# A gated recurrence and eight capped experts in one kernel: a new order for the last third of the stream, five units gated by GpSimd and TensorE, and three zero fills held back

## The chip, the cores and the metric

The kernel runs on one core of a Trainium2 chip. The metric is the device time of one execution in microseconds.

## What is computed

The first half is a gated linear recurrence over 4 sequences of 5056 tokens with 256 channels, the second a mixture of experts that takes the result as tokens (20224 x 256).

```python
log_a = c * sig_r * np.log(np.clip(a_base, 1e-06, 1.0 - 1e-06))[None, None, :]
a_t = np.exp(log_a)
norm = np.sqrt(np.maximum(1.0 - a_t * a_t, 1e-06))
x_gated = norm * sig_i * x
for t in range(S):
    h = a_t[:, t] * h + x_gated[:, t]
    y[:, t] = h
...
logits = x @ w_gate
expert_idx = np.argmax(logits, axis=1)
...
out = np.zeros((N, D), dtype=np.float32)
for e in range(E):
    ...
    h = np.maximum(x[tok_idx] @ w1[e], 0.0)
    out[tok_idx] = gate_w[tok_idx, None] * (h @ w2[e])
```

Each expert takes at most 80 of its tokens, those of the largest gate weight. So all but 640 rows at most of the output are zeros, and they have to be written too.

## The kernel before

**The stream.** The tokens are cut into 40 units of 512 (the last has 256). For each unit three blocks of 512 KB are loaded (tokens `Lr`, `Li`, `Lx` of the order for r_gate, i_gate and x), turned so that channels lie on partitions, and scanned. A unit goes through these steps: `Tr` transposes r on TensorE into PSUM; `tr` takes its tanh on ScalarE; `e` is the decay exp(...) on ScalarE, two instructions, one for each half of the channels; `q` squares it on GpSimd; `s` takes the root on ScalarE; `ti` is the tanh of half of i, so that the sigmoid is (1 + ti) / 2; the gating makes (1 + ti) times x, either on VectorE in one instruction (`v`, line 159) or on GpSimd in two (`u`, lines 156 and 157: add one, then multiply); `Tu` transposes the product into a PSUM tile `pu`, one for each half of the channels, four matmuls with the identity as the moving operand; `xg` multiplies it with the root on VectorE (line 167); `y` is the scan on VectorE (line 175). A digit behind a point names a half for `Tu`, `xg` and `y`, and for the others how many units one instruction takes together (`e32.2` takes units 32 and 33).

**Slots.** One large tile Y has 50 slots of 4 KB on each partition. The scans fill slots 0 to 39 for good, one for each unit; until then these and slots 40 to 49 hold what is loaded and the decays. `SLOTS` names the slot of each block. A load can't start before the last reader of what lay in its slot: for r that is `xg`, for x `Tu`, for i the gating, for a decay `y`.

**The order.** `ORDER` is one list, written out by hand, of all steps. Each engine issues its own steps in the order of this list, and SyncE its transfers: the loads, the zero fills `Z` and the weights `W`. A step that waits holds back all that stands behind it on its engine. The transfers of SyncE go to the same 16 DMA engines in the order of issue.

**Zero fills.** 40 fills of 512 KB (the last has half) write zeros to the output. All but the first copy from the part of the output that is already zero, so they read and write HBM. All 40 stand in `ORDER`; line 407 asks for what may be left, which is nothing.

**Routing.** `G` makes the logits of four units (16 matmuls), `R s.k` are the steps of routing group s (maximum, exp, key, sum, reciprocal, gate weight, store). `P` takes the largest cells of a stretch, `M` merges them. `M0` (line 349) also replaces the eight largest and finds the next eight. `F` are matmuls that only keep TensorE running.

**Weights.** Slots 40 to 47 become the buffers of two experts' weights. `W0` to `W3` load the halves of w1 of experts 0 and 1, `W4` to `W7` those of w2. In the list W0 comes first, then W7, W3, W6, W5, W4, W2 and W1, with four fills between them; nine fills stand behind W1.

**Selection and experts.** After line 407 the 80 best tokens of each expert are chosen, mostly on VectorE. `experts()` then runs a loop over k from -1 to 7: in step k TensorE makes the first products of expert k + 1 (line 629) and the second ones of expert k (line 631), in two halves of the inner dimension. Behind each half SyncE issues the next weights of the buffers just read: `load_w1(e1 + 2, half)` and `load_w2(e2 + 2, half)`. The w1 of expert 2 is first used in step 1, its w2 and the w1 of expert 3 in step 2.

Of the kernel before, what the change touches and what calls it, by code (L numbers as in the profile page):

```python
# [13 lines left out]
ALU = mybir.AluOpType  # L14
# [14 lines left out]
SLOTS = dict(r=(14, 25, 30, 35, 38, 18, 21, 16, 34, 9, 11, 20, 13, 26, 25, 37, 42, 45, 40, 48, 41, 49, 22, 31, 24, 30, 44, 45, 41, 46, 49, 35, 32, 37, 42, 46, 44, 45, 41, 46),  # L29
             i=(34, 40, 4, 27, 37, 44, 23, 37, 28, 19, 15, 23, 32, 18, 46, 49, 38, 16, 21, 30, 28, 25, 26, 34, 37, 32, 43, 36, 38, 31, 36, 30, 41, 45, 36, 43, 49, 37, 38, 49),  # L30
             x=(20, 12, 29, 22, 40, 24, 6, 42, 36, 29, 27, 35, 41, 24, 36, 17, 29, 18, 27, 43, 33, 38, 47, 42, 33, 28, 32, 27, 34, 38, 33, 34, 48, 33, 38, 48, 40, 43, 40, 47),
             a=(15, 8, 31, 19, 33, 5, 14, 7, 17, 10, 30, 12, 28, 34, 14, 23, 35, 38, 19, 20, 27, 35, 23, 29, 25, 26, 40, 47, 28, 29, 43, 31, 40, 47, 34, 35, 36, 42, 48, 39))
# [51 lines left out]
def moe_kernel(ctx, tc, x, r_gate, i_gate, a_param, w_gate, w1, w2, out, capacity=80):  # L84
# [129 lines left out]
    for k in range(6): nc.gpsimd.memset(tiny[:, 70 + k % 4:71 + k % 4], 0.0)  # L214
# [171 lines left out]
    def weights(w):  # L386
# [4 lines left out]
             'Tr': r_transposes, 'tr': r_tanh, 'e': decay, 'q': square, 's': root, 'ti': i_tanh, 'u': gated, 'v': gated,  # L391
# [15 lines left out]
    zero_fill(-(-N // ZERO_TOKENS))  # L407
# [180 lines left out]
    def experts(arm):  # L588
        fstack = ExitStack()
# [31 lines left out]
        def products(e1, e2, half):  # L621
# [17 lines left out]
            if e1 is not None and e1 + 2 < E: load_w1(e1 + 2, half)  # L639
            if e2 is not None and e2 + 2 < E: load_w2(e2 + 2, half)  # L640
# [80 lines left out]
```

## Time and profile before

| | |
|---|---|
| time, median of 3 runs | 292.08 us (287.35 to 293.74) |
| the profiled execution's own time | 287.59 us |
| its span, first to last instruction | 285.9 us |
| mean granted TensorE clock, share of full speed | 0.915 |
| busy: VectorE, ScalarE, GpSimd, TensorE | 223.0, 232.9, 213.0, 211.1 us |
| DMA, mean rate over the span | 352 GB/s |

The shares are means over three stages that have different limits: the stream to about 201 us, the selection to about 223 us and the experts to the end. PE is TensorE's matmuls, PEld its weight loads, DVE VectorE, ACT ScalarE, POOL GpSimd, SP SyncE. A clock of 1.00 is 2.4 GHz, 0.50 is 1.2 GHz.

### The profile page before, as it was taken

The numbers are of one execution on the slowest core, as the hardware profiler recorded it, in microseconds if no ns is written. First come the engines' busy times: TensorE is split into PE (matmuls) and PEld (weight loads), VectorE is DVE, ScalarE is ACT, GpSimd is POOL, SyncE is SP. The second block draws the span as 40 slices with busy tenths as digits, with TensorE's granted clock in tenths as the row PEclk, the third lists the DMA queues.
The fourth block names the chain that finished last, engine by engine and source line by source line (L and its number), as shares of the span: only waits on it lengthen the run. The fifth ranks groups of instructions, "written<-read, shape, count | busy, mean of one in ns | idle before, by whom it ended". The sixth has DMA issues, their size and how long they took to land.

```text
span 285.9 us, 5799 instructions
## 1 busy us (share of the span) xinstructions
PE 211.1 (74%) x1488; PEld 161.0 (56%) x1488; DVE 223.0 (78%) x506; ACT 232.9 (81%) x488; POOL 213.0 (75%) x372
## 2 busy tenths in 40 slices
PE   2635849598556985479857696486787889999995
PEld 2634723375444354462555325333676779999994
DVE  2018999999999999999999999999995663445510
ACT  7999999999999999999999999999264754544400
POOL 3279488789999999999999788998375682816521
PEclk9995977689959999779979997979999997999999
DMA  6999999999999999999889999999999997999831
GB/s 232 417 386 416 410 408 408 409 391 396 411 405 436 367 367 359 386 344 413 318 318 396 353 406 387 410 364 344 304 408 406 347 297 240 342 340 331 299 93 32
DMA packets 32825, 100.74 MB, mean 352 GB/s; under 512 B 3744, under 2 KB 12576, under 8 KB 32160
## 3 DMA queue, kind: packets, MB, share of 16 engines
q1 hardware_dynamic: 32400, 99.64, 93.1%
q0 software_dynamic: 384, 0.66, 0.7%
q8 instruction: 14, 0.23, 0.3%
q14 instruction: 27, 0.22, 0.2%
HBM read 99.10 MB, written 21.36 MB: 421 GB/s over the span
## 4 chain that ended last, share of the span: by engine, by line
DMA 29%; PE 21%; DVE 17%; POOL 12%; ACT 8%; issue 8%; SPq 2%; ACTq 1%; DVEq 0%; POOLq 0%
DMA Y<-in_x_dram 11%; PE po L631 9%; PE ph L629 7%; DVE Y L175 6%; POOL Y L157 6%; DMA Y<-in_i_gate_dram 6%; DMA Y<-in_r_gate_dram 6%; DMA Y<-in_moe_w_dram 4%; POOL Y L145 3%; DVE Y L159 3%; DMA Y<-in_moe_w_gate_dram 3%; DVE pu L167 3%; POOL Y L156 2%; ACT Y L142 2%; SPq L120 2%
## 5 line engine op out<-in xcount | busy, mean ns | idle before, releaser
L175 DVE TENSOR_TENSOR_SCAN Y<-Y,pu 128x512 f32<-128x512 f32 (+4 forms) x86 | 97.9, 1171 | 0.4
L164 PE MATMUL pu<-ident,Y 128*128 128x128 f32 x316 | 53.7, 303 | 49.0 <-DVE Y L175 26.0
L145 POOL TENSOR_TENSOR Y<-Y 128x1024 f32<-128x1024 f32 (+2 forms) x29 | 74.5, 2589 | 18.8 <-ACT Y L142 17.6
L164 PEld LDWEIGHTS pu<-ident,Y 128*128 128x128 f32 x316 | 38.7, 154 | 71.3 <-issue 37.9
L157 POOL TENSOR_TENSOR Y<-Y 128x1024 f32<-128x1024 f32 (+1 forms) x23 | 57.4, 2498 | 1.9
L128 PE MATMUL pr<-ident,Y 128*128 128x128 f32 x316 | 50.1, 313 | 11.5 <-DMA Y<-in_r_gate_dram 8.2
L128 PEld LDWEIGHTS pr<-ident,Y 128*128 128x128 f32 x316 | 43.5, 165 | 16.4 <-issue 6.7
L167 DVE SCALAR_TENSOR_TENSOR pu<-Y,pu 128x512 f32<-128x512 f32 (+1 forms) x80 | 51.2, 673 | 0.6 <-ACT Y L148 0.2
L142 ACT ACTIVATE Y<-Y,tiny 128x1024 f32<-128x1024 f32 (+2 forms) x48 | 49.5, 1089 | 0.1
L631 PE MATMUL po<-Y,rows 128*80 128x128 f32 x256 | 46.9, 279 | 0.0
L629 PE MATMUL ph<-Y 128*128 128x80 f32 x256 | 43.1, 263 | 2.7 <-DMA Y<-in_moe_w_dram 1.8
L629 PEld LDWEIGHTS ph<-Y 128*128 128x128 f32 x256 | 38.1, 196 | 3.4 <-POOL Y L617 3.3
L152 ACT ACTIVATE Y<-Y 128x1024 f32<-128x1024 f32 (+2 forms) x30 | 39.6, 1328 | 0.4 <-DMA Y<-in_i_gate_dram 0.3
L130 ACT ACTIVATE Y<-pr 128x1024 f32<-128x1024 f32 (+1 forms) x40 | 39.4, 1009 | 0.1
L616 ACT COPY Y<-Y 128x2 f32 x256 | 25.8, 191 | 16.7 <-issue 14.2
L148 ACT ACTIVATE Y<-Y 128x2048 f32<-128x2048 f32 (+2 forms) x26 | 37.5, 1493 | 0.4 <-POOL Y L145 0.2
L159 DVE SCALAR_TENSOR_TENSOR Y<-Y 128x1024 f32<-128x1024 f32 (+1 forms) x16 | 23.8, 1500 | 16.2 <-DMA Y<-in_moe_w_gate_dram 10.1
L617 POOL COPY Y<-Y 128x2 f32 x192 | 24.6, 195 | 14.7 <-DVE Y L646 5.7
L238 PE MATMUL pl<-Y 128*32 128x512 f32 x144 | 34.1, 1077 | 0.5 <-DVE Y L175 0.5
L156 POOL TENSOR_SCALAR Y<-Y 128x1024 f32<-128x1024 f32 (+1 forms) x23 | 26.6, 1158 | 6.0 <-ACT Y L152 5.7
L631 PEld LDWEIGHTS po<-Y,rows 128*80 128x80 f32 x256 | 29.2, 155 | 0.0
L643 DVE TENSOR_SCALAR rows<-ph 128x320 f32<-128x320 f32 x8 | 3.9, 492 | 27.1 <-PE ph L629 24.0
(165 smaller groups left out, 200.3 us busy)
## 6 DMA issues: line engine op xcount, KB each, us to landing
Y<-in_r_gate_dram SPq DMA_DIRECT2D x39, 512.0 KB, 6.9
Y<-in_i_gate_dram SPq DMA_DIRECT2D x39, 512.0 KB, 7.2
Y<-in_x_dram SPq DMA_DIRECT2D x39, 512.0 KB, 7.7
out_dram<-out_dram SPq DMA_DIRECT2D x38, 512.0 KB, 9.6
Y<-in_moe_w_dram SPq DMA_DIRECT2D x32, 512.0 KB, 6.9
out_dram<-Y SPq DMA_DIRECT2D x1, 512.0 KB, 10.4
Y<-in_x_dram SPq DMA_DIRECT2D x1, 256.0 KB, 5.7
Y<-in_i_gate_dram SPq DMA_DIRECT2D x1, 256.0 KB, 5.1
```

Of the source, the lines that this page charges most:

```text
L128: nc.tensor.transpose(pr[:, h, b:nb * P:nb], rr[:, b, h * P:(h + 1) * P], ident)
L130: nc.scalar.activation(rslot(u), prs.pop(u)[:, :, :ntok(u)], AF.Tanh, scale=0.5)
L142: nc.scalar.activation(a[:, :, h], z[:, :, h], AF.Exp, scale=L[:, h:h + 1], bias=L[:, h:h + 1])
L145: nc.gpsimd.tensor_tensor(pair('r', u, m), a, a, op=ALU.mult)
L148: nc.scalar.activation(q, q, AF.Sqrt, scale=-0.25, bias=0.25)
L152: nc.scalar.activation(i, i, AF.Tanh, scale=0.5)
L157: nc.gpsimd.tensor_tensor(v, i, v, op=ALU.mult)
L164: nc.tensor.transpose(pu[:, b:nb * P:nb], tmb('x', u)[:, b, h * P:(h + 1) * P], ident)
L167: nc.vector.scalar_tensor_tensor(pu, rslot(u)[:, h], 0.5e-3, pu, op0=ALU.max, op1=ALU.mult)
L175: nc.vector.tensor_tensor_scan(y[:, s0:s1], a[:, s0:s1], q[:, s0:s1], init, op0=ALU.mult, op1=ALU.add)
L629: if e1 is not None: nc.tensor.matmul(ph[:, c % (FC // 2)], w1v(e1)[:, h, c * P:c * P + P], XG[:, e1, h], start=(h == 0), stop=(h == 1))
L631: if e2 is not None: nc.tensor.matmul(po[:, h, :P], h2T[:, c], w2v(e2)[:, c, h * P:h * P + P], start=(c == 0), stop=(c == FC - 1))
```

## The change

The list is the same up to unit 26. Behind it all steps of units 27 to 39 are in a new order, and 39 of the slots are others; of those, r36 goes to slot 47, x36 to 41 (behind x34), x38 to 44, r39 to 47 (behind r36), i39 to 41 (behind x36) and x39 to 48 (behind i37).

Units 30, 32, 34, 36 and 38 are gated by a new step `w`: GpSimd multiplies ti with x in one instruction, and `Tu` sums the transposes of x and of that product in PSUM, eight matmuls a half in place of four. Before, four of these units were gated by GpSimd (`u`) and unit 34 by VectorE (`v34.1`).

The decays of units 37 and 38 and the roots of 35 and 36 are made together (`e37.2`, `s35.2`). The step `R4.4` moves behind the last scan, and `M4` takes over the replacing and the second search from `M0`, behind `R5.2`.

Of the 40 fills 33 stand in the list, four follow at line 407, and three wait until the first weights of expert 2 have been issued: one behind the first half, two (the half-size one is among them) behind the second. The weights come in the order W0, W4, W5, W2, W1, W3, W6, W7. Six more one-column memsets stand at the start of GpSimd's work.

```diff
@@
 GATHER = (32, 24, 24)
 STEPS = ((0, 1), (2, 3), (4, 5), (6, 7), (8,), (9,))
...
@@
-    Tu27.1 xg26.1 y26.0 y26.1 xg27.1 Lr32 Tu27.0 Lr36 Lx30 xg27.0 Tr31 s29.2 Tu28.1 R2.4 s28.1 y27.1 y27.0 Li33 Z R2.5 xg28.1 Tu28.0 Tr32 xg28.0
-    Tu29.1 y28.1 Lx31 tr31 y28.0 Li32 u30.1 R2.6 xg29.1 Z R2.7 tr32 Tr33 Tu29.0 e31.1 xg29.0 Tu30.0 Tr36 y29.1 tr33 Lr35 ti31.1 e32.2 y29.0 R2.8
-    Tu30.1 v31.1 q31.1 ti32.2 q32.2 Li34 Lx34 xg30.0 R2.9 Tu31.0 xg30.1 Lx33 Tr35 Li36 y30.0 Z s31.1 y30.1 P2 s32.2 Z xg31.0 tr35 Li35 Tu31.1
-    u32.1 xg31.1 u33.1 ti34.1 G6 Lr38 y31.0 Tu32.0 Tu32.1 e34.2 y31.1 Lx35 xg32.0 xg32.1 y32.0 Z G7 Tu33.0 tr36 v34.1 R3.0 q34.2 ti35.2 y32.1
-    Tu33.1 xg33.0 xg33.1 e36.1 q36.1 R3.1 R3.2 Lr37 R3.3 y33.1 v35.1 s34.1 Z Z Lx36 Tu34.0 y33.0 R3.4 R3.5 Li37 u36.1 xg34.0 Tu34.1 xg34.1 Tr37
-    s35.1 s36.1 tr37 ti37.1 Lx37 y34.0 Tu35.1 Tu35.0 Tr38 Lx39 e37.1 y34.1 xg35.1 R3.6 Z R3.7 R3.8 xg35.0 y35.1 tr38 Li38 u37.1 R3.9 y35.0 e38.1
-    Tu36.1 P3 Tu36.0 Z Li39 Z Lr39 G8 ti38.1 xg36.1 Tu37.1 xg36.0 y36.1 y36.0 q37.1 q38.1 s37.1 Lx38 Z xg37.1 R4.0 Tu37.0 s38.1 R4.1 xg37.0 R4.2
-    R4.3 y37.0 Tr39 ti39.1 u38.1 Tu38.1 Z Z Z Z y37.1 Z u39.1 Z tr39 e39.1 q39.1 R4.4 Tu38.0 I0 xg38.1 Ga0 Z xg38.0 W0 Z s39.1 y38.1 y38.0 Tu39.0
-    Tu39.1 xg39.1 R4.5 xg39.0 W7 y39.1 Z Ga1 W3 W6 W5 W4 Z Z Ca y39.0 Gb F R5.0 R4.6 M0 R5.1 W2 R4.7 W1 Z Z R4.8 M1 M3 Z F F F F F R5.2 F F F F I1 Z Z Z R4.9 Z R5.3 Z
-    R5.4 Z R5.5 R5.6 R5.7 R5.8 F F F F F F F F M2 R5.9
+    Tu27.1 xg26.1 y26.0 xg27.1 Tu27.0 y26.1 Tu28.0 xg27.0 Tr33 Li32 y27.1 s28.2 R2.4 R2.5 xg28.0 y27.0 s30.1 y28.0 Tu28.1 ti31.1 Tr31 R2.6 Lx30
+    Lr32 Tu29.0 Lx31 tr31 Li33 xg28.1 Lr36 R2.7 Tu29.1 xg29.1 xg29.0 R2.8 w30.1 tr33 e31.1 y28.1 q31.1 Tr32 tr32 R2.9 Tu30.0 e32.2 Lx34 ti32.2
+    y29.0 Tu30.1 q32.2 xg30.0 v31.1 y30.0 G6 s31.1 y29.1 xg30.1 Tu31.1 Tu31.0 Tr36 Lr35 Z Lx33 y30.1 Tr35 Li36 Li34 Z w32.1 xg31.1 xg31.0 u33.1
+    s32.2 tr35 y31.1 ti34.1 y31.0 Tu32.0 Tu32.1 G7 xg32.0 e34.2 tr36 Li35 w34.1 R3.0 Z Lx35 xg32.1 y32.0 y32.1 Tu33.1 Tu33.0 q34.2 Tu34.0 ti35.2
+    R3.1 Li37 P2 xg33.1 xg33.0 Z Lr37 y33.1 Tu34.1 e36.1 R3.2 v35.1 Lr38 Lx36 R3.3 y33.0 Lx37 R3.4 s34.1 xg34.1 q36.1 xg34.0 Tu35.0 R3.5 R3.6
+    y34.0 Tr37 R3.7 Tr38 Tu35.1 s35.2 Z ti37.1 y34.1 xg35.0 xg35.1 Z y35.0 w36.1 tr37 R3.8 tr38 Tu36.1 R3.9 e37.2 Li38 u37.1 ti38.1 Z Lx38 y35.1 Z
+    q37.1 Tu36.0 xg36.1 G8 xg36.0 Tu37.0 s37.1 q38.1 y36.1 Lr39 R4.0 y36.0 s38.1 P3 Li39 ti39.1 Tu37.1 Lx39 xg37.0 Z Z xg37.1 y37.0 Tr39 tr39
+    w38.1 Z R4.1 Z Z Tu38.1 R4.2 y37.1 xg38.1 Z Tu38.0 Ga0 xg38.0 u39.1 y38.1 e39.1 Tu39.0 W0 q39.1 Tu39.1 s39.1 W4 y38.0 xg39.0 R4.3 Z Ga1 xg39.1
+    y39.0 Z y39.1 I0 Ca Gb F R5.0 R4.4 R4.5 R4.6 M0 R5.1 W5 W2 W1 W3 R4.7 R5.2 Z Z R4.8 M1 M4 M3 Z F F F F F F F F F I1 Z Z Z R4.9 R5.3 Z R5.4 Z
+    R5.5 R5.6 R5.7 R5.8 F F F F F F F F W6 W7 M2 R5.9
 """
 EARLY = 8
+HELD = (1, 2)
 class Plan:
@@
         for token in ORDER.split():
             kind = token.rstrip("0123456789.")
             self.order.append((kind, *map(int, filter(None, token[len(kind):].split(".")))))
-        self.by_pool = {u + k for kind, *a in self.order if kind == 'u' for u in a[:1] for k in range(a[1])}
+        self.by_pool, self.summed = ({u + k for kind, *a in self.order if kind == g for u in a[:1] for k in range(a[1])} for g in 'uw')
         self.steps = STEPS
         self.step_of = {g: s for s, gs in enumerate(STEPS) for g in gs}
@@
             nc.gpsimd.tensor_tensor(v, i, v, op=ALU.mult)
         else:
             nc.vector.scalar_tensor_tensor(v, i, 1.0, v, op0=ALU.add, op1=ALU.mult)
+    def times_tanh(u, m):
+        ti, v = flat_pair('i', u, m), flat_pair('x', u, m)
+        nc.gpsimd.tensor_tensor(ti, ti, v, op=ALU.mult)
     def u_transposes(u, h):
+        terms = [tmb(k, u) for k in ('xi' if u in plan.summed else 'x')]
         pu = pus[u, h] = ps_u.tile([P, C], F32, name="pu")
         nb = ntok(u) // P
         for b in range(nb):
-            nc.tensor.transpose(pu[:, b:nb * P:nb], tmb('x', u)[:, b, h * P:(h + 1) * P], ident)
+            for n, v in enumerate(terms):
+                nc.tensor.matmul(pu[:, b:nb * P:nb], v[:, b, h * P:(h + 1) * P], ident, start=(n == 0), stop=(n == len(terms) - 1), is_transpose=True)
     def normed(u, h):
         n = ntok(u); pu = pus[u, h][:, :n]
         nc.vector.scalar_tensor_tensor(pu, rslot(u)[:, h], 0.5e-3, pu, op0=ALU.max, op1=ALU.mult)
@@
     cidx = tiny[:, 38:70]; ecol = tiny[:, 22:38]
     nc.gpsimd.iota(cell0, pattern=[[2 * P, 4]], base=0, channel_multiplier=0, allow_small_or_imprecise_dtypes=True)
     warm = tiny[:, 21:22]
-    for k in range(6): nc.gpsimd.memset(tiny[:, 70 + k % 4:71 + k % 4], 0.0)
+    for k in range(12): nc.gpsimd.memset(tiny[:, 70 + k % 4:71 + k % 4], 0.0)
     dio = tiny[:, 4:20]
     for e in range(2 * E): nc.gpsimd.memset(dio[:, e:e + 1], float(E - e % E))
@@
             nc.gpsimd.iota(nth, pattern=[[1, NC]], base=0, channel_multiplier=0, allow_small_or_imprecise_dtypes=True)
             best(0)
             find(0)
+        if n == 4:
             nc.vector.match_replace(cell, rows[:, NE:NE + 8], cell, -1.0)
             best(8)
         pool = nc.gpsimd
@@
         load(e, g)
     tasks = {'Lr': lambda u: load('r', u, rf), 'Li': lambda u: load('i', u, jf), 'Lx': lambda u: load('x', u, xf),
-             'Tr': r_transposes, 'tr': r_tanh, 'e': decay, 'q': square, 's': root, 'ti': i_tanh, 'u': gated, 'v': gated,
+             'Tr': r_transposes, 'tr': r_tanh, 'e': decay, 'q': square, 's': root, 'ti': i_tanh, 'u': gated, 'v': gated, 'w': times_tanh,
              'Tu': u_transposes, 'xg': normed, 'y': scan, 'G': logits, 'R': lambda s, k: stages[k](s), 'Ga': logits_first, 'Gb': logits_last, 'Ca': copy_first, 'P': cell_top, 'M': merge, 'I': prepare, 'W': weights, 'Z': lambda: zero_fill(1), 'F': filler}
     with tc.manual_schedule(engines={E_.Activation, E_.PE, E_.DVE, E_.Pool}):
         for n, (kind, *args) in enumerate(plan.order):
@@
     sel = bank[:5 * E, :CAP]
     tstack = ExitStack()
     ps_t = tstack.enter_context(tc.tile_pool(name="ps_t", bufs=1, space=bass.MemoryType.PSUM))
-    zero_fill(-(-N // ZERO_TOKENS))
+    zero_fill(-(-(N - nz[0]) // ZERO_TOKENS) - sum(HELD))
+    filled = nz[0]
     KG, KF = -(-CAP // 8) * 8, 14
     chosen = small[:5 * E, 0:CAP]
@@
     _, fv = nc.values_load_multi_w_load_instructions(flag, engines=[E_.PE, E_.DVE, E_.Activation, E_.Pool, E_.SP], min_val=0, max_val=P,
                                                      skip_runtime_bounds_check_because="a count of rows")
     def experts(arm):
+        nz[0] = filled
         fstack = ExitStack()
         tstack = ExitStack()
         ps_t = tstack.enter_context(tc.tile_pool(name="ps_a" + arm, bufs=1, space=bass.MemoryType.PSUM))
@@
             for c in cs[len(lone):]:
                 for h in range(2): first(c, h); second(c, h)
             if e1 is not None and e1 + 2 < E: load_w1(e1 + 2, half)
+            if e1 == 0: zero_fill(HELD[half])
             if e2 is not None and e2 + 2 < E: load_w2(e2 + 2, half)
         def relu(e, half):
             dst = hbuf[e % 2].rearrange("p (c s) -> p c s", c=FC)[:, half * FC // 2:(half + 1) * FC // 2]
```

## Rows read from the trace of the kernel before

**Rows 1.** Stage windows: busy us of PE, PEld, DVE, ACT, POOL; clock, DMA share, GB/s.

```profile
160.00:170.00 10.00, 9.16 (x52) 3.07 (x52) 9.97 (x14) 9.94 (x10) 9.36 (x5) 1.00 0.98 383
230.00:240.00 10.00, 8.21 (x67) 8.01 (x67) 6.58 (x57) 5.15 (x49) 4.79 (x38) 0.85 0.98 321
260.00:270.00 10.00, 10.00 (x101) 10.00 (x100) 4.71 (x40) 5.83 (x54) 6.98 (x43) 1.00 0.99 330
```

**Rows 2.** Chain of waits, 215 us to the end: start, us, what.

```profile
225.67 10.57 DMA Y<-in_moe_w_dram
```

**Rows 3.** TensorE timeline around the experts' first matmuls; in brackets the idle time before.

```profile
223.66 1.98 PE L629 MATMUL ph<-Y 128*128 128x80 f32 x16 [0.94 <-ACT Y L616]
...
236.38 0.42 PE L629 MATMUL ph<-Y 128*128 128x80 f32 x2 [1.79 <-DMA Y<-in_moe_w_dram]
```

**Rows 4.** Two-microsecond windows, columns as in the first group.

```profile
222.00:224.00 2.00, 1.06 (x7) 0.66 (x6) 1.32 (x12) 1.67 (x18) 0.85 (x7) 1.00 1.04 369
238.00:240.00 2.00, 2.00 (x12) 2.00 (x12) 0.42 (x4) 0.00 (x0) 0.00 (x0) 0.50 0.93 323
```

**Rows 5.** SyncE timeline: start, us, line, transfers issued.

```profile
185.47 0.33 SPq L120 DMA_DIRECT2D Y<-in_x_dram  x1
185.86 6.10 SPq L230 DMA_DIRECT2D out_dram<-out_dram  x8
196.84 0.39 SPq L381 DMA_DIRECT2D Y<-in_moe_w_dram  x1
...
211.42 12.57 SPq L230 DMA_DIRECT2D out_dram<-out_dram  x9
225.67 5.86 SPq L381 DMA_DIRECT2D Y<-in_moe_w_dram  x3
231.62 0.88 SPq L384 DMA_DIRECT2D Y<-in_moe_w_dram  x1
...
241.28 0.37 SPq L381 DMA_DIRECT2D Y<-in_moe_w_dram  x1
...
244.52 0.37 SPq L381 DMA_DIRECT2D Y<-in_moe_w_dram  x1
```

**Rows 6.** DMA issues at 185.47, 196.84, 225.67, 231.62 us; last number: us to landing.

```profile
Y<-in_x_dram SPq DMA_DIRECT2D x1, 512.0 KB, 6.0
...
Y<-in_moe_w_dram SPq DMA_DIRECT2D x1, 512.0 KB, 9.4
...
Y<-in_moe_w_dram SPq DMA_DIRECT2D x1, 512.0 KB, 10.6
...
Y<-in_moe_w_dram SPq DMA_DIRECT2D x1, 512.0 KB, 8.6
```

**Rows 7.** VectorE timeline, 168 to 196 us.

```profile
169.20 1.41 DVE L159 SCALAR_TENSOR_TENSOR Y<-Y 128x1024 f32<-128x1024 f32 x1
...
194.56 0.28 DVE L300 SCALAR_TENSOR_TENSOR pl<-pl,tiny 128x128 f32<-128x128 f32 x1
```

**Rows 8.** GpSimd timeline, 160 to 168 us.

```profile
162.44 1.05 POOL L156 TENSOR_SCALAR Y<-Y 128x1024 f32<-128x1024 f32 x1
163.57 2.42 POOL L157 TENSOR_TENSOR Y<-Y 128x1024 f32<-128x1024 f32 x1
```

**Rows 9.** TensorE timeline, 185 to 196 us.

```profile
185.99 3.81 PE L238 MATMUL pl<-Y 128*32 128x512 f32 x16 [0.54 <-DVE Y L175]
...
194.31 1.09 PE L164 MATMUL pu<-ident,Y 128*128 128x128 f32 x8 [2.31 <-POOL Y L157]
```

**Rows 10.** ScalarE groups by form, 130 to 201 us: count, busy, mean ns.

```profile
L142 ACT ACTIVATE Y<-Y,tiny 128x512 f32<-128x512 f32 x10 | 7.6, 810 | 0.0
```

**Rows 11.** GpSimd groups by form, first 10 us: count, busy, mean ns, idle before.

```profile
L145 POOL TENSOR_TENSOR Y<-Y 128x1024 f32<-128x1024 f32 x1 | 1.9, 1892 | 7.0 <-ACT Y L142 7.0
...
L214 POOL MEMSET tiny<- 128x1 f32 x6 | 0.3, 88 | 0.0
```

**Rows 12.** Page, under the DMA queues.

```profile
HBM read 99.10 MB, written 21.36 MB: 421 GB/s over the span
```

More of the change, by code (lines that the diff above doesn't have):

```diff
@@ L28 @@
 STEPS = ((0, 1), (2, 3), (4, 5), (6, 7), (8,), (9,))
[L29 to L32, printed above, removed]
+SLOTS = dict(r=(14, 25, 30, 35, 38, 18, 21, 16, 34, 9, 11, 20, 13, 26, 25, 37, 42, 45, 40, 48, 41, 49, 22, 31, 24, 30, 44, 45, 41, 46, 37, 43, 48, 49, 42, 46, 47, 40, 45, 47),
+             i=(34, 40, 4, 27, 37, 44, 23, 37, 28, 19, 15, 23, 32, 18, 46, 49, 38, 16, 21, 30, 28, 25, 26, 34, 37, 32, 43, 36, 38, 33, 35, 38, 32, 33, 37, 35, 38, 48, 42, 41),
+             x=(20, 12, 29, 22, 40, 24, 6, 42, 36, 29, 27, 35, 41, 24, 36, 17, 29, 18, 27, 43, 33, 38, 47, 42, 33, 28, 32, 48, 31, 36, 45, 31, 34, 45, 41, 43, 41, 37, 44, 48),
+             a=(15, 8, 31, 19, 33, 5, 14, 7, 17, 10, 30, 12, 28, 34, 14, 23, 35, 38, 19, 20, 27, 35, 23, 29, 25, 26, 40, 47, 28, 29, 30, 36, 40, 44, 34, 36, 49, 43, 46, 39))
 ORDER = """
```

## Prediction

> **What bounds the kernel now.** I read the stage windows first, then the chain of waits, then the place it points to on TensorE, SyncE and the DMA rings. In the stream VectorE and ScalarE are busy for 9.97 and 9.94 of 10 us, GpSimd for 9.36, and the DMA share is 0.98, so four things are nearly full together and an edit to one of them can be eaten by the next [rows 1]. In the last experts TensorE is busy without a gap while the DMA engines move 330 GB/s at the pace at which TensorE frees the weight buffers [rows 1]. Between the two lies the only long DMA piece of the chain's last third: 10.57 us from 225.67 us [rows 2]. It is the first half of expert 2's w1, issued when TensorE has read expert 0's. TensorE needs it at 236.38 - 1.79 = 234.59 us and waits 1.79 us [rows 3]. Then the clock stands at 0.50, 1.2 GHz, in the window 238 to 240 us, although it was 1.00 around the shorter idle time of 0.94 us before the first product [rows 3, 4]. SyncE's issues mark the ends of the halves: the half that began at 236.38 ended at 241.28 (4.90 us), the next at 244.52 (3.24 us) [rows 3, 5]. So the low clock cost 4.90 - 3.24 = 1.66 us. **Wait and clock together cost 3.45 us**, and that is what holding fills back aims at.
>
> The weight comes late because of what is queued ahead of it: nine fills, issued over 12.57 us from 211.42 us [rows 5]. I price the queue by landings, issue plus time to landing [rows 5, 6]: x38, the last load, 185.47 + 6.0 = 191.5; W0 196.84 + 9.4 = 206.2; the weight in question 225.67 + 10.6 = 236.3; the first half of expert 2's w2 231.62 + 8.6 = 240.2. Between the last two only weights run, the last included three: 3.9 / 3 = **1.3 us a weight**. Between x38 and W0 lie eight fills and one weight: (14.7 - 1.3) / 8 = 1.68 us a fill. Between W0 and 236.3 lie eight weights and 12.5 fills: (30.1 - 10.4) / 12.5 = 1.58. I take **1.6 us a fill**.
>
> **The change: the stream.** VectorE loses `v34`, 1.41 us [rows 7]. GpSimd loses four additions of 1.05 and gains one product of 2.42, 1.8 us less in sum [rows 8]. ScalarE loses part of four decay instructions of 0.81 us, at most two of them, 1.6 us, and at least nothing [rows 10]. TensorE gets 5 x 8 = 40 more transposes; eight take 1.09 us, so 5.5 us over some 40 us [rows 9]. It has the time: it stood waiting 2.31 us for GpSimd's product before one such group [rows 9]. On the path, behind a product that comes late, each half costs 1.09 / 2 = 0.55 us more. `M4` and the three instructions of `R4.4` (0.28 us for the first) only move on VectorE, to where it is the bound anyway; I cost them at nothing, and at 0.9 us if VectorE was idle where `R4.4` stood, since it filled a gap before `xg38` there [rows 7]. The six memsets cost 6 x 0.088 = 0.5 us of GpSimd before its first product, where it idles 7.0 us: nothing [rows 11].
>
> So the stream can end 1.4 us earlier at best. Against that stand three new waits. `R3.6` now stands right behind `xg34`, before GpSimd has surely finished `R3.5`. `G8`'s 3.81 us stand on TensorE before `Tu37`, and VectorE has only `y36` and `P3` to fill them [rows 9]. A `w` has nothing to do before x has landed, while the addition in `u` needed only ti. The bounds are a gain of 1.4 and a loss of 0.6 us: two halves of `Tu` uncovered, 1.1, and the 0.9 of `R4.4`'s gap, against the 1.4. I take a gain of 0.6: 1.4 less one uncovered half, 0.55, less the first 0.28 of that gap. Nothing in the selection changes, so TensorE needs expert 2's first weight at 234.0 us.
>
> **The fills and the weights.** What counts is what runs after the last load. Before: 8 + 12.5 fills and nine weights to the end of the weight in question. After: six fills ahead of W0, then two, eight and four, 20 in all, and the same nine weights. Only half a fill less, 0.8 us, although three are held back: the list has seven fills fewer, but the four of line 407 still come ahead of the weight, and they were taken out of the stream. The rest of the saving, two fills, lies ahead of the last load, and it counts only if the DMA engines don't run dry there. The two bounds: all 2.5 fills count, 236.3 - 2.5 x 1.6 = 232.3; or the last load lands when it did, 236.3 - 0.8 = 235.5. I take **235.0**, near the second, because the last load is now x39, whose slot is freed by GpSimd's `u37` and not by the queue, with r39 and i39 waiting for unit 36 just ahead of it on SyncE. So the first wait is 235.0 - 234.0 = 1.0 us, close to the 0.94 us that left the clock alone, and I count no low clock for it.
>
> Then the held fills are due: one behind the first half, 1.5 behind the second. Expert 2's w2 lands behind 2.5 fills and three weights, 235.0 + 4.0 + 3.9 = 242.9. TensorE would be there at 235.0 + 2 x 3.24 = 241.5, so **a new wait of 1.4 us** takes the place of the old one. Step 2 starts at 242.9 and started at 244.52. From there on TensorE's pace decides as before. The first scatter has to follow the held fills, and GpSimd's copies for a later expert stand behind it on that engine; the fills land ahead of expert 2's w2, in time for both. The sum: 242.9 - 244.52 = -1.6 us on 287.59 us (span 285.9, 1.7 around it): **286.0 us**. If the clock falls in the second wait, it is 1.66 us more, 287.6. The median shown, 292.08, is 4.5 us above the profiled execution and the shortest run (287.35); my sum stands on the profiled one, and runs like the median's would put the change near 290.5.
>
> A word on the price of a fill. The row says 421 GB/s of HBM traffic, read and written, over the whole span [rows 12]. The Trainium skill, "DMA: Bandwidth & Descriptors", section Specifications, gives about 358 GB/s as the limit of HBM for one core and says that this side binds. By that, a fill that reads and writes 0.52 MB each would take 1.05 MB / 358 GB/s = 2.9 us, an estimate from the page, and my sum would get 2.5 x 1.3 = 3.3 us longer. The trace goes past that limit, so the row decides.
>
> **The rivals.** *Both waits gone.* The queue never runs dry: the weight lands at 232.3, and expert 2's w2 at 232.3 + 7.9 = 240.2; the stream gives its whole 1.4 us, TensorE is ready at 233.2 and at 239.7 and waits 0.5 us at most. 240.2 - 244.52 = -4.3: 283.3 us. For it speaks the DMA share of 0.98 in the stream, against it that loads wait for slots, not for the queue [rows 1]. *Nothing gained.* The first wait stays near 1.5 us or the second comes to as much, the clock falls, 287.6 us. The change then doesn't do what its words say: the fills are held back, but only as many as were put off from the list into the stretch ahead of the weight. *Slower: late x.* x36 now takes slot 41, freed by the second `Tu34`, where it had one that was free after a scan two units earlier. GpSimd's `w36` waits for it, with `u37`, `q37`, `q38`, `w38` and `u39` queued behind, x39 waits for `u37`, and on SyncE all last fills and weights wait behind x39. Loads took 6.0 us to land there and up to 10.6 under a full queue [rows 6]. If x36 lands 3 us after GpSimd has come to `w36`, stream and weight both move by 3 us: 286.0 + 3.0 = 289.0 us. It decides from 1.6 us on, where the gain is used up. *Dear fills.* Beside weights a held fill could cost more than in a run of fills; at 2.9 us each step 2 starts 3.3 us later, 289.3 us.
>
> **How the numbers follow.** Forecast 286.0 (284.5 to 287.2) 0.42; both waits gone 0.22; nothing gained 0.18; late x 0.13; dear fills 0.05. The range reaches from below the second to above the fourth, with the median's distance in view: 282.5 to 290.5. Two per cent, 5.8 us, is about what a measurement here can tell from no change, since the three runs lie 6.4 us apart. Faster by more needs 281.8: only a tail of the second case and the scatter of the runs, 0.15. Slower by more needs 293.3: 0.06. Within: 0.79.
>
> **What would show it.** In the profile after: the 1.79 us wait of line 629 before step 1 shrinks to about 1 us or goes, with no stretch at 0.50 behind it; a wait for line 384's or 381's load appears before step 2; the weight behind the fills lands near 235 us; VectorE's last scan ends 0.2 to 1.4 us earlier. I am wrong if the first product of the experts starts later than 223.7 us (then the stream lost), if no wait stands before step 2 (then fills are cheaper or the queue ran ahead), or if the clock is low for more than the 1.66 us.

## Result: 1.1 per cent slower, where 0.6 per cent faster was forecast

The changed kernel takes 289.9 us (median of 20 runs, 288.15 to 292.27), the kernel before in the same series 289.19 us (median of 20, 286.25 to 294.71). The ratio is **1.0108, 95% interval 1.0085 to 1.0131**; it is larger than that of the medians because disturbed runs, of which the kernel before had more, are left out of it. The profiled execution took 290.63 us, 3.0 us more than the one before, where 1.6 us less was forecast.

**The profile after.** The stage windows answer to [rows 1]. In the stream VectorE is busy for 9.70 of 10 us in place of 9.97 and GpSimd for 9.92 in place of 9.36; where the experts start, TensorE is busy for 6.46 in place of 8.21.

```profile
160.00:170.00 10.00, 9.51 (x64) 4.78 (x56) 9.70 (x12) 9.94 (x9) 9.92 (x5) 1.00 0.96 354
230.00:240.00 10.00, 6.46 (x55) 6.26 (x54) 6.46 (x57) 5.16 (x49) 4.81 (x38) 0.86 0.98 335
260.00:270.00 10.00, 10.00 (x102) 10.00 (x101) 6.87 (x52) 5.15 (x49) 7.37 (x50) 1.00 1.04 337
```

The rest is read from the end of the stream to the start of the experts. VectorE's timeline first, one row of before and four of after: the last scan started 0.68 us earlier, but the three instructions of `R4.4`, which had stood ahead of `xg38`, now stand behind it.

```profile
199.61 1.38 DVE L175 TENSOR_TENSOR_SCAN Y<-Y,pu 128x256 f32<-128x256 f32 x2
...
198.93 1.38 DVE L181 TENSOR_TENSOR_SCAN Y<-Y,pu 128x256 f32<-128x256 f32 x2
200.22 0.27 DVE L306 SCALAR_TENSOR_TENSOR pl<-pl,tiny 128x128 f32<-128x128 f32 x1
200.53 0.29 DVE L307 TENSOR_REDUCE Y<-pl 128x16 f32<-128x128 f32 x1
200.85 0.29 DVE L308 TENSOR_TENSOR lg<-pl,Y 128x128 f32<-128x128 f32 x1
```

What follows `R4.4` on VectorE started at 201.06 us, so `R4.4` took 0.84 us; before, the same instruction started at 200.90, so the gain was given back. TensorE's timeline shows the first product of the experts 0.05 us earlier than in [rows 3], and the wait that was to shrink is twice as long:

```profile
223.61 1.98 PE L638 MATMUL ph<-Y 128*128 128x80 f32 x16 [0.92 <-ACT Y L625]
...
238.09 0.69 PE L638 MATMUL ph<-Y 128*128 128x80 f32 x2 [3.54 <-DMA Y<-in_moe_w_dram]
```

In the chain of waits the weight is one DMA piece, as in [rows 2], 1.76 us longer:

```profile
225.62 12.33 DMA Y<-in_moe_w_dram
```

SyncE's timeline, to compare with [rows 5]: the last load, the fills (line 236), the weights (388 w1, 391 w2), and, from 244.21 us on, the issues that mark the ends of the experts' halves.

```profile
188.33 0.33 SPq L121 DMA_DIRECT2D Y<-in_x_dram  x1
188.71 4.62 SPq L236 DMA_DIRECT2D out_dram<-out_dram  x6
195.64 0.39 SPq L388 DMA_DIRECT2D Y<-in_moe_w_dram  x1
196.13 0.43 SPq L391 DMA_DIRECT2D Y<-in_moe_w_dram  x1
196.61 1.21 SPq L236 DMA_DIRECT2D out_dram<-out_dram  x2
197.92 0.53 SPq L391 DMA_DIRECT2D Y<-in_moe_w_dram  x1
199.20 2.88 SPq L388 DMA_DIRECT2D Y<-in_moe_w_dram  x3
203.67 11.37 SPq L236 DMA_DIRECT2D out_dram<-out_dram  x8
216.26 2.15 SPq L391 DMA_DIRECT2D Y<-in_moe_w_dram  x2
219.60 4.62 SPq L236 DMA_DIRECT2D out_dram<-out_dram  x4
225.62 0.37 SPq L388 DMA_DIRECT2D Y<-in_moe_w_dram  x1
...
233.53 0.37 SPq L391 DMA_DIRECT2D Y<-in_moe_w_dram  x1
...
244.21 0.37 SPq L388 DMA_DIRECT2D Y<-in_moe_w_dram  x1
...
247.44 0.37 SPq L388 DMA_DIRECT2D Y<-in_moe_w_dram  x1
```

The half behind the wait runs from 238.09 to 244.21, 6.12 us in place of 3.23 for the next, so the low clock cost 2.89 us, against 1.66 before. Two-microsecond windows (columns of [rows 1]) show it: 0.50, 1.2 GHz, after TensorE had stood idle for 3.54 us.

```profile
238.00:240.00 2.00, 1.91 (x10) 1.94 (x11) 0.40 (x4) 0.00 (x0) 0.00 (x0) 0.50 1.06 412
240.00:242.00 2.00, 2.00 (x12) 2.00 (x12) 0.00 (x0) 0.00 (x0) 0.00 (x0) 0.50 0.94 358
242.00:244.00 2.00, 2.00 (x13) 2.00 (x12) 0.00 (x0) 0.00 (x0) 0.17 (x1) 0.50 0.75 274
244.00:246.00 2.00, 2.00 (x21) 2.00 (x21) 0.00 (x0) 1.72 (x16) 1.65 (x7) 0.99 0.73 214
```

**The account:** first product -0.05, wait 3.54 - 1.79 = +1.75, low clock 2.89 - 1.66 = +1.23: +2.9 of the 3.0 us. The landings behind it, in the form of [rows 6], for the issues at 188.33 (x39), 195.64 (W0), 225.62 and 233.53 us:

```profile
Y<-in_x_dram SPq DMA_DIRECT2D x1, 256.0 KB, 4.2
...
Y<-in_moe_w_dram SPq DMA_DIRECT2D x1, 512.0 KB, 8.0
...
Y<-in_moe_w_dram SPq DMA_DIRECT2D x1, 512.0 KB, 12.3
...
Y<-in_moe_w_dram SPq DMA_DIRECT2D x1, 512.0 KB, 11.6
```

x39 landed at 192.5 us, W0 at 203.6, the weight at 237.9. Between the last two lie 14 fills and eight weights, at the prediction's 1.3 us a weight (34.3 - 10.4) / 14 = 1.71 us a fill.

Ahead of x39 the DMA engines had room. SyncE issued nothing from 181.56 to 187.08 us, since r39's slot wasn't free; before, the longest pause in the 25 us ahead of x38 was 3.45 us. Windows of before, of after and of experiment 3, which has four fills more ahead of x39; the last two figures are DMA share and GB/s:

```profile
172.00:186.00 14.00, 7.65 (x48) 6.18 (x50) 13.90 (x20) 13.94 (x16) 12.34 (x11) 0.87 0.98 390
...
172.00:186.00 14.00, 8.99 (x60) 7.67 (x58) 13.90 (x20) 13.94 (x14) 12.14 (x10) 0.88 0.92 334
...
172.00:186.00 14.00, 9.98 (x61) 9.21 (x60) 13.90 (x20) 13.94 (x15) 10.66 (x10) 0.76 0.99 404
```

In the windows of two microseconds in it the share of after swings between 0.64 and 1.37. So the engines didn't stand still throughout, but over these 14 us they moved 0.8 MB less than before, 1.5 fills.

### The profile page after: what moved, and what is told of

The parts are those of the page before. It is cut to its first block, busy times and chain, and to the rows that moved or that the text cites. A ratio compares the mean times of both kernels' runs of the same rounds, so it can differ in the third digit from the quotient of the medians.

```text
span 288.9 us, 5876 instructions
## 1 busy us (share of the span) xinstructions
PE 217.7 (75%) x1528; PEld 168.3 (58%) x1528; DVE 222.2 (77%) x505; ACT 232.4 (80%) x485; POOL 211.2 (73%) x375
## 4 chain that ended last, share of the span: by engine, by line
PE 23%; DMA 21%; POOL 18%; DVE 18%; issue 11%; ACT 6%; SPq 2%; ACTq 1%; POOLq 0%; DVEq 0%
DMA Y<-in_x_dram 9%; PE po L640 9%; PE ph L638 7%; POOL Y L146 6%; DVE Y L181 5%; POOL Y L158 5%; DMA Y<-in_moe_w_dram 4%; DVE pu L173 4%; DVE Y L160 3%; DMA Y<-in_moe_w_gate_dram 3%; DMA Y<-in_i_gate_dram 3%; PE pl L244 3%; POOL Y L157 2%; PE pu L170 2%; POOL Y L163 2%
## 5 line engine op out<-in xcount | busy, mean ns | idle before, releaser
L181 DVE TENSOR_TENSOR_SCAN Y<-Y,pu 128x512 f32<-128x512 f32 (+5 forms) x86 | 98.2, 1172 | 0.5
L170 PE MATMUL pu<-ident,Y 128*128 128x128 f32 x356 | 59.6, 305 | 47.8 <-DVE Y L181 24.3
L170 PEld LDWEIGHTS pu<-ident,Y 128*128 128x128 f32 x356 | 44.3, 156 | 70.5 <-issue 37.2
L129 PEld LDWEIGHTS pr<-ident,Y 128*128 128x128 f32 x316 | 44.2, 167 | 12.3 <-issue 6.0
L158 POOL TENSOR_TENSOR Y<-Y 128x1024 f32<-128x1024 f32 (+1 forms) x19 | 47.9, 2520 | 1.6
L143 ACT ACTIVATE Y<-Y,tiny 128x1024 f32<-128x1024 f32 (+2 forms) x46 | 48.8, 1122 | 0.1
L638 PE MATMUL ph<-Y 128*128 128x80 f32 x256 | 44.0, 268 | 4.5 <-DMA Y<-in_moe_w_dram 3.5
L638 PEld LDWEIGHTS ph<-Y 128*128 128x128 f32 x256 | 39.0, 200 | 5.1 <-issue 3.7
L160 DVE SCALAR_TENSOR_TENSOR Y<-Y 128x1024 f32<-128x1024 f32 (+1 forms) x15 | 22.8, 1531 | 15.9 <-DMA Y<-in_moe_w_gate_dram 10.1
L157 POOL TENSOR_SCALAR Y<-Y 128x1024 f32<-128x1024 f32 (+1 forms) x19 | 22.4, 1178 | 6.6 <-ACT Y L153 5.3
```

What stands on the lines that cost most here:

```text
L129: nc.tensor.transpose(pr[:, h, b:nb * P:nb], rr[:, b, h * P:(h + 1) * P], ident)
L143: nc.scalar.activation(a[:, :, h], z[:, :, h], AF.Exp, scale=L[:, h:h + 1], bias=L[:, h:h + 1])
L170: nc.tensor.matmul(pu[:, b:nb * P:nb], v[:, b, h * P:(h + 1) * P], ident, start=(n == 0), stop=(n == len(terms) - 1), is_transpose=True)
L181: nc.vector.tensor_tensor_scan(y[:, s0:s1], a[:, s0:s1], q[:, s0:s1], init, op0=ALU.mult, op1=ALU.add)
L638: if e1 is not None: nc.tensor.matmul(ph[:, c % (FC // 2)], w1v(e1)[:, h, c * P:c * P + P], XG[:, e1, h], start=(h == 0), stop=(h == 1))
```

## The experiments

**Theory A, the queue:** the list has seven fills fewer. Three of them had stood behind W0 and are held back now. Four had stood ahead of W0, in the stream, where the DMA engines now have room; they come at line 407, in the stretch ahead of expert 2's first weight, and holding back three (2.5 by size) doesn't make up for these four. (The expectation of 1 speaks of seven fills taken out of the stream; by the lists it is four.) Rivals: **B**, the new order or the gating loses; **C**, W6 and W7, now last, delay the weight; **D**, only the first weight counts, so more held fills would cure it. Times are told by the ratio to the kernel before on the same chip. From each profiled execution I take one number that leaves the stream out, product to end: span less the start of the experts' first product (all in us).

| kernel | ratio to before (95%) | first product | span | product to end |
|---|---|---|---|---|
| before | 1 | 223.66 | 285.9 | 62.2 |
| after | 1.0108 (1.0085 to 1.0131) | 223.61 | 288.9 | 65.3 |
| 1 held alone | 0.9887 (0.9812 to 0.9963) | 224.19 | 285.9 | 61.7 |
| 1 again | 0.9916 (0.9871 to 0.9962) | 225.27 | 283.8 | 58.5 |
| 2 none held | 1.0172 (1.0114 to 1.0231) | 224.11 | 291.6 | 67.5 |
| 3 four back | 0.9949 (0.9915 to 0.9982) | 224.68 | 283.1 | 58.4 |
| 3 again | 0.9945 (0.9901 to 0.9988) | 226.40 | 284.8 | 58.4 |
| 4 three back | 0.9924 (0.9881 to 0.9967) | 225.01 | 283.5 | 58.5 |
| 5 seven held | 1.0101 (1.0037 to 1.0164) | 223.99 | 289.9 | 65.9 |
| 6 W6, W7 early | 1.0058 (1.0015 to 1.0101) | 224.42 | 290.3 | 65.9 |
| 7 kept busy, 28 | 1.0110 (1.0072 to 1.0148) | 224.33 | 288.8 | 64.5 |
| 8 kept busy, 14 | 1.0020 (0.9971 to 1.0068) | 223.71 | 287.7 | 64.0 |
| 9 old gating | 1.0155 (1.0064 to 1.0246) | 232.10 | 293.7 | 61.6 |
| 10 held, warmer | 0.9926 (0.9879 to 0.9972) | 229.38 | 287.8 | 58.4 |

**1. Three fills held back in the kernel before, and nothing else.** The list loses three `Z` at its end.

```diff
+HELD = (1, 2)
...
+            if e1 == 0: zero_fill(HELD[half])
```

Expected: 

> The kernel before with nothing but the held fills: the last three of its nine fills behind W1 leave the list and go behind the halves of expert 2's w1, as in the change. Theory A (the queue decides: the change lost because its list gave seven fills out of the stream into the stretch ahead of expert 2's first weight, and holding three back doesn't make up for that): the weight lands 2.5 x 1.6 = 4.0 us earlier, near 232.3 us, TensorE doesn't wait for it, no window at 0.50 follows, and the time falls by the whole 3.45 us of wait and low clock, to about 284 us in a run like the profiled one. Theory B (the new order and gating of the stream cost the time, the fills matter little): within 1 us of the kernel before.

Measured: 287.16 us (median of 6), before 288.38; -1.1 per cent, as A has it. No wait for a weight was left: the first half of expert 2's w1 was issued at 226.20 and landed 6.4 us later. But the clock fell all the same, in the second half of step 0 and without a long wait ahead of it (TensorE, then windows; the same 16 matmuls take 2.01 us at full clock):

```profile
224.19 1.98 PE L632 MATMUL ph<-Y 128*128 128x80 f32 x16 [0.78 <-ACT Y L619]
...
226.34 3.42 PE L632 MATMUL ph<-Y 128*128 128x80 f32 x16
```

```profile
228.00:230.00 2.00, 2.00 (x12) 2.00 (x12) 0.65 (x6) 1.40 (x15) 0.80 (x7) 0.50 0.84 262
230.00:232.00 2.00, 2.00 (x11) 2.00 (x11) 1.80 (x16) 0.88 (x9) 2.00 (x17) 0.50 0.77 268
```

**1 again**, on another chip. Expected: 

> The kernel before with the three held fills once more, for the comparison with two more keep-running matmuls on the same chip: the ratio to the kernel before again near 0.989, times spread over 4 to 5 us. If the clock's fall at 228 us is a matter of one execution, this profile shows 1.00 there, and its span is 2 to 2.5 us shorter than 285.9.

Measured: 286.43 us (12 runs), before 288.77. This profile has no low clock there, and 58.5 us from product to end, 3.2 less than the first:

```profile
228.00:230.00 2.00, 2.00 (x20) 2.00 (x20) 1.73 (x16) 2.00 (x21) 0.97 (x8) 1.00 0.80 217
```

So the fall belongs to single executions, not to this kernel; 58.4 to 58.5 us is the price of the experts when nothing waits and the clock holds.

**2. The change with no fill held back**, `HELD = (0, 0)`, so that seven stand at line 407. Expected: 

> The changed kernel with all seven fills issued ahead of expert 2's first weight, none held back. A: the weight lands 2.5 x 1.7 = 4.3 us later than in the changed kernel, near 242 us, the wait grows from 3.5 to about 7.8 us, the time by 4 us, to about 294. B: no change beyond 1 us.

Measured: 293.54 us (6 runs). TensorE's wait:

```profile
242.23 0.69 PE L638 MATMUL ph<-Y 128*128 128x80 f32 x2 [7.26 <-DMA Y<-in_moe_w_dram]
```

Three fills more ahead of the weight, one of them half-size, put it 4.1 us later, 1.7 us for a full one. A's place and size hold.

**3. The change with the four fills of line 407 back in the stream**, where the engines had room: one behind `Lr36`, two behind `Lr38`, one behind the last fill ahead of `Lr39`. Of each line only the place that differs:

```diff
-    Lr36 R2.7
+    Lr36 Z R2.7
...
-    Lr38 Lx36 R3.3
+    Lr38 Z Z Lx36 R3.3
...
-    Lx38 y35.1 Z
+    Lx38 y35.1 Z Z
```

Expected: 

> The changed kernel with the four fills of line 407 put back into the list of the stream: one behind Lr36, two behind Lr38, one behind the last fill before Lr39; three stay held. A: there the DMA engines had gaps, so the last loads come at most 1 us later, and the weight lands 4 x 1.7 - 1 = 5.8 us earlier, near 232.2 us; the wait of 3.54 us and the 2.9 us of low clock both go, and the time falls to about 283.5 us, under both kernels. B: the fills get in the way of the loads of units 36 to 39, the stream ends later, and the time stays at 290 us or more.

Measured: 285.88 us (12 runs), before 288.38. The weight was issued at 226.70 and landed at 231.7, 6.2 us earlier than in the change, no product waited for it, and the clock was 1.00 from 214 to 252 us:

```profile
Y<-in_moe_w_dram SPq DMA_DIRECT2D x1, 512.0 KB, 5.0
```

x39, issued at 188.33 as in the change, took 6.7 us and not 4.2, and the first product came 1.07 us later. That the four fills cost this is not shown: in 5, with no fill put back, x39 took 6.8 us, and in 6, whose stream is the change's, the first product came 0.81 us later than in the change.

**3 again**, on the chip of 4 and 10. Expected: 

> The version with four fills put back into the stream once more, on the chip of the two versions that are made from it and beside it: the ratio to the kernel before again near 0.995, first product again near 224.7 us with x39 landing 6 to 7 us after its issue, no wait for expert 2's weights. If the lateness of the first product belonged to one execution, it is back near 223.7 us here.

Measured: 286.6 us (12 runs), the same ratio. The first product came at 226.40, a miss, but some 1.0 us of that is again a fall of the clock: the matmuls that keep TensorE running ahead of it took 6.24 us here, 4.55 in 3 and 4, and the idle time behind them shrank from 0.92 to 0.22 us. The same fall stands in the profiles of 2 (6.24) and 7 (6.14). From product to end it is 58.4 us.

```profile
219.94 6.24 PE L447 MATMUL pd<-Y,ident 128*128 128x256 f32 x20 [0.75 <-DVE Y L547]
226.40 1.98 PE L638 MATMUL ph<-Y 128*128 128x80 f32 x16 [0.22 <-DMA Y<-in_moe_w_dram]
```

**4. Three back**, the one behind `Lx38` left at line 407. Expected: 

> The version with four fills put back into the stream, without the one right behind x38: three are back, the fourth stays at line 407. Theory A (fills count in the queue where they stand): in the version with four back, x39 landed 6.7 us after its issue, against 4.2 us in the changed kernel, and the first product of the experts came 1.07 us later. Without that fill x39 has one transfer less ahead of it, 1.3 to 1.7 us, so the first product is back near 223.7 us. Expert 2's first weight has one fill more between x39 and itself and still lands by 233.5 us, under TensorE's need at 234.0, so no wait over 0.9 us and no low clock. About 1 us under the version with four back on the same chip. Rival: the lateness of 1.07 us comes from the three other fills or from the run, then the first product stays at 224.7 us and the time is the same.

Measured: 285.76 us (12 runs), on the chip of "3 again". No wait for expert 2's weights, and with 285.76 against 286.6 and intervals that overlap nothing tells the two apart. The first product stayed late, at 225.01, so the rival holds: the microsecond comes from the three other fills, or varies by as much between executions, for which 6 speaks; it isn't this fill.

**5. Seven held**, `HELD = (3, 4)`. Expected: 

> The changed kernel with all seven fills held back, three behind the first half of expert 2's w1 and four behind the second, none at line 407. A: that weight lands 4 x 1.7 = 6.8 us earlier, near 231 us, and its wait goes; but expert 2's w2 still has all 40 fills ahead of it and lands where it did, near 245 us, while TensorE now wants it at 241 us: a wait of about 4 us before step 2, with a low clock behind it, so most of the gain is given back, 287 to 290.5 us. Theory D (only the wait for the first weight matters): the whole 6.4 us are gained, 283.5 us.

Measured: 291.68 us (6 runs). Nothing waits ahead of step 1, but then

```profile
245.48 0.69 PE L638 MATMUL ph<-Y 128*128 128x80 f32 x2 [4.09 <-DMA Y<-in_moe_w_dram]
...
246.92 0.68 PE L640 MATMUL po<-Y,rows 128*80 128x128 f32 x2 [0.76 <-DMA Y<-in_moe_w_dram]
```

and the clock stood at 0.50 from 244 to 250 us. D is out: past the first weight the same queue stands ahead of the next.

This run also answers 3, since up to W7 its list is the change's, and between W0 and the weight both have ten fills: the four that 3 has in the stream wait behind the weight here. x39, issued at 188.54, and the weight, issued at 226.01 us:

```profile
Y<-in_x_dram SPq DMA_DIRECT2D x1, 256.0 KB, 6.8
...
Y<-in_moe_w_dram SPq DMA_DIRECT2D x1, 512.0 KB, 6.0
```

x39 landed at 195.3 us (in 3 at 195.0), W0 at 205.9 (205.4), the weight at 232.0 (231.7). So in this pair four fills in the stream delayed none of these; the same four at line 407 put the weight 6 us later.

**6. W6 and W7 issued right behind W3.** Expected: 

> The changed kernel with W6 and W7 issued right behind W3, ahead of the eight fills, in place of behind them. Theory A (length of the queue since W0): the same 14 fills and eight weights lie ahead of expert 2's first weight, it lands within 0.5 us of 238.0, the time stays within 1 us. Theory C (the late W6 and W7 hold it up, by standing right before it): it lands 2.6 us earlier, at 235.4, and the time falls by 2.6 us or more.

Measured: 290.31 us (10 runs). The fills left as one block of 12 at 209.23 us, and the weight was no earlier:

```profile
239.55 0.68 PE L638 MATMUL ph<-Y 128*128 128x80 f32 x2 [4.20 <-DMA Y<-in_moe_w_dram]
```

It landed at 239.4, 1.5 us later than in the change and not within the 0.5 us expected; 1.2 us of that stand already at x39's issue, at 189.53. C is out: what stands ahead of the weight counts, not the place of W6 and W7 in it.

**7. The change with 28 matmuls more behind step 0**, identity by identity into a spare PSUM tile, to keep TensorE busy during the wait. Expected: 

> The changed kernel with 28 matmuls of the identity on TensorE behind step 0 (about 3.1 us at the rate of the 16 at the end), where it waits 3.54 us for the weight. It changes nothing about the queue. If the low clock comes from that idle time, the clock stays at 1.00, the half after the wait takes 3.24 us in place of 6.12, and the time falls by 2.9 us to about 287 us, with the weight landing where it did. If the low clock has another cause, the time stays or grows by up to 3 us.

Measured: 290.28 us (12 runs). The size was wrong: each is two records, so they ran far past the landing. But the half behind them took 241.28 to 244.48 us, 3.20, full pace:

```profile
235.02 6.42 PE L693 MATMUL bank<-ident 128*128 128x128 f32 x56
241.28 0.35 PE L638 MATMUL ph<-Y 128*128 128x80 f32 x2
```

**8. The same with 14.**

```diff
+            if k == 0:
+                for _ in range(14): nc.tensor.matmul(bank[:, :P], ident, ident, start=True, stop=True)
```

Expected: 

> The changed kernel with 14 identity matmuls behind step 0. The 28 of the run before stood in the trace as 56 records and took 6.42 us, so they ended 3.2 us after the weight had landed and ate what the clock gave. 14 should take 3.2 us and end about when the weight lands, near 238 us. If the low clock comes from the idle time, the half after it takes 3.24 us in place of 6.12 and the time falls by 2.9 us against the changed kernel, to about 287 us. If it doesn't, the time stays at 290.

Measured: 289.03 us (12 runs), ratio 1.002, 0.9 per cent or some 2.5 us under the change.

```profile
234.47 3.29 PE L693 MATMUL bank<-ident 128*128 128x128 f32 x28
...
238.62 0.42 PE L638 MATMUL ph<-Y 128*128 128x80 f32 x2 [0.86 <-DMA Y<-in_moe_w_dram]
...
246.52 0.42 PE L640 MATMUL po<-Y,rows 128*80 128x128 f32 x2 [0.71 <-DMA Y<-in_moe_w_dram]
```

The clock was 1.00 from 226 to 252 us, so the low clock is bought by the idle time: the half behind the wait took 3.28 us, 238.62 to 241.90. And at full pace the second wait of the prediction appears: 0.71 us in step 2, for a w2. Such waits take part of the gain back, so in the profiles product to end is 1.3 us shorter than in the change (64.0 and 65.3).

**9. The change's order and slots with the old gating**, `u30 u32 v34 u36 u38` in place of the five `w`. Expected: 

> The changed kernel with the old gating in the new order and the new slots: units 30, 32, 36 and 38 by GpSimd in two instructions, unit 34 by VectorE. Up to u37 GpSimd has 3 x 1.05 - 2.42 = 0.8 us more to do, VectorE 1.2 to 1.4. A: x39, W0 and the weight come about 1 us later, the last scan 0.8 to 1.4 us later, the time grows by about 1 us. Theory B1 (the new gating with its double transposes is what loses): the first product of the experts comes earlier than 223.6 us and the time falls by 1 us or more.

Measured: 294.16 us (4 runs). The first product came at 232.10, 8.5 us later; 2.4 of these stood already at the `P` step of 130.7 us (here 133.06), ahead of where the lists differ, so at most 6.1 belong to the edit. GpSimd waited longer where it had waited 0.72 and 0.81 us in the change:

```profile
180.35 1.89 POOL L146 TENSOR_TENSOR Y<-Y 128x1024 f32<-128x1024 f32 x1 [3.24 <-ACT Y L143]
...
187.29 0.63 POOL L322 TENSOR_TENSOR lg<-lg,Y 128x256 f32<-128x256 f32 x1 [2.66 <-DVE Y L320]
```

More than the 1 us expected, so the size was wrong; the part of B that blames the gating is out, since the new order depends on it.

**10. Experiment 1 with two more keep-running matmuls ahead of the first product**, `WARM = (13, 12)`. Expected: 

> The kernel before with the three held fills, and two more of the matmuls that only keep TensorE running just ahead of the experts' first product, to cover its 0.8 to 0.9 us of idle time. In the profiled execution of the version without them the clock stood at 0.50 from 228 to 234 us although no long wait stood there. If the idle time ahead of the first product is the cause: clock 1.00 from 226 to 236 us, a smaller spread than 284.3 to 289.1 us, and a median about 2 us under that version's on the same chip. Rival: the fall comes from something else, then the clock falls here too and the times spread as before.

Measured: 286.54 us (12 runs), 286.43 for 1 on the same chip, ranges 284.2 to 290.1 and 283.9 to 293.0. The idle time ahead of the first product went from 0.95 to 0.21 us and brought nothing. The clock was 1.00 from 222 us on, but so it was in "1 again". This profiled execution lost 4 us in the stream, where the clock stood at 0.50 for the ten microseconds from 180 us, with TensorE busy for 7.37 of them. The rival holds.

## Why the prediction was wrong

**What bounds the kernel: right.** The wait for expert 2's first weight and the low clock behind it were priced at 3.45 us. With both gone the part from product to end is 58.4 to 58.5 us in five executions, 3.7 to 3.8 under the 62.2 of before.

**The step that failed** is the landing: "I take **235.0**, near the second", between 232.3 and 235.5. It was 237.9, outside both, and 237.6, 238.5 and 239.4 in 7, 8 and 6, which have the same 20 fills behind the last load. I had found that the list has seven fills fewer and that 20 fills, where there were 20.5, still lie between the last load and the weight; by this count alone 0.8 us was saved. Then I took half a microsecond off for the two fills ahead of the last load, and held 235.5 for an upper end. It wasn't one. Against 235.5, three terms: x39 landed at 192.5, x38 had landed at 191.5, +1.0; 14 fills cost 1.71 each and not 1.58, +1.8; six fills ahead of W0 cost (11.1 - 1.3) / 6 = 1.63 and not 1.68, -0.3. That is, to rounding, the 2.4 us by which it missed the bound. The two fills taken out ahead of the last load were worth nothing: x39 was issued at 188.33 us with 17 fills ahead of it, at 188.33 with 21 (3) and at 188.36 with 20 (4), so the slots set the time, as the prediction had feared, and not the fills (in "3 again", with the list of 3, it was 191.02). Experiments 2, 3 and 5 show the cause: three fills more between W0 and the weight move it by +4.1 us, four fewer by -6.2 and -5.9, and whether these four stand in the stream (3) or behind the weight (5) changes its landing by 0.3. The median, 289.9 us, lies inside the stated range of 282.5 to 290.5, which was made that wide for the scatter of the runs; the path to it was another.

**The clock** follows from that step. I counted none for a wait of 1.0 us; 3.54 us of idle time were followed by 2.89 us of loss. Experiments 7 and 8 give the low clock back with no earlier weight (3.20 and 3.28 us for the half behind the wait, in place of 6.12).

**The second wait** of 1.4 us didn't come: w2 landed at 233.53 + 11.6 = 245.1, and TensorE, slowed by the clock, needed it at 247.44. The mechanism was right and showed where the clock held (8: 0.71 us) or more was held (5: 4.09).

**The stream** was forecast 0.6 us shorter. The last scan was 0.68 earlier, and the first product 0.05: the failed term is `R4.4`, costed at 0.28 with 0.9 as its bound; it cost 0.84. Both are read from one pair of executions: in 2, 5, 6, 7 and 8, whose stream is the change's, the last scan started between 198.43 and 199.73 us, before at 199.61. With four or three fills back in the stream the first product came at 224.68 and 225.01, later than the bound of a loss of 0.6 us allows (224.26); but so it did in 6 (224.42), so the fills aren't shown to be the reason. *Late x*, the rival on the slower side, had the direction but not the place: x39 landed 1.0 us later, and GpSimd waited for an x for only 0.29 us. *Nothing gained* named the reason, as many fills put off as held back, with less than half of the wait that came. *Dear fills* took 2.9 us a fill, which no run shows: behind W0 it was 1.57 to 1.71 (see Open). *Both waits gone* is what the versions 3 and 4 became.

**What each part is worth,** by the ratios: three fills held in the old order, 0.9887 and 0.9916; the new order with those held and three or four back, 0.9924 to 0.9949. So holding back brings about 1 per cent, the new order and gating nothing that can be measured, and the four fills moved from the stream to line 407 cost 1.6 to 1.8 (1.0108 against 0.9949 and 0.9924). The versions 1, 3 and 4 beat both kernels.

**The price of a fill:** the Trainium skill, "DMA: Bandwidth & Descriptors", section Specifications, has some 358 GB/s as the limit of HBM for one core. That this side binds, as the prediction puts it, is said by the page's section "Where 436 GB/s comes from", and of transfers between HBM and SBUF, which a fill is not. Here the rows decide: by the page of each profile the kernel after read and wrote 417 GB/s over its span, experiment 3 426, and these count a fill twice, as read and as written. Section Bandwidth of the same page gives 425 GB/s for the largest transfers of a core whose neighbour idles, a figure near these.

**Open:** why a fill cost 1.65 to 1.71 us behind W0 where 14 stand between it and the weight (the change, 7, 8), 1.57 to 1.60 where ten do (1, 3, 5), and 1.58 before, with 12.5. And why the clock fell in single executions of 1, 2, 7 and "3 again" while TensorE had been at work with no gap over 1.03 us shortly before. The last of these gaps, ahead of the first product, doesn't decide it: in 2, 7 and "3 again" the fall came ahead of it, and "1 again", with 0.95 us there in place of 0.78, kept the clock.

## What to carry to other kernels

A transfer taken out of one stretch must be followed to where it lands: what decides is how many stand between the last load that sets its own pace and the first weight that is needed, and a place where loads wait for their slots, and not for the queue, gives nothing back when it is emptied further. Hold back what can wait, but no more than fits ahead of the next need: three fills behind the first weights gained 1 per cent, seven moved the wait one step on. And split the span at the first product: product to end scattered by 0.1 us between the executions with no wait and no low clock in it, the first product by more than 2.

## What the runs showed of the hardware

The clock fell to 1.2 GHz for 6 us in experiment 1 with TensorE busy from 224.19 us on and idle times of 0.78 to 1.03 us before; another execution of the same kernel, with 0.95 us before the product, kept 2.4 GHz. One fp32 matmul of the identity with itself is two records of 0.12 us each (56 records, 6.42 us). A weight's time from issue to landing says how long the queue is, and little of the weight: 5.0 us in experiment 3, 12.3 in the change, for the same 512 KB.
